# A shared pool of eight PSUM banks, and exp on VectorE for some score banks, in a fused attention and gated-MLP kernel

## The chip, the cores and the metric

The kernel runs on one core of a Trainium2 chip. The metric is device time in microseconds (us); lower is better. The engines are named as in the profile: PE is TensorE, ACT is ScalarE, DVE is VectorE, POOL is GpSimd, SP issues most of the DMAs. In the profile PE's weight loads stand under their own name, PEld, and overlap with PE.

## The reference

One pre-LN block, in bf16, for 2048 tokens of width 1024: attention with 32 query heads of width 32 that share one key and one value head, then a gated MLP of width 3584.

```
def _A_ref(x, wq, wk, wv, wo):              # H = 32 heads, Dh = 32
    q = (x @ wq).reshape(B, S, H, Dh).transpose(0, 2, 1, 3)
    k = x @ wk ; v = x @ wv                 # one head each
    p = softmax(einsum("bhqd,bkd->bhqk", q, k) * Dh ** -0.5)
    o = einsum("bhqk,bkd->bhqd", p, v)
    return o.transpose(0, 2, 1, 3).reshape(B, S, H * Dh) @ wo
def _B_ref(x, w_gate, w_up, w_down):
    return (sigmoid(x @ w_gate) * (x @ w_up)) @ w_down
h  = x + _A_ref(layernorm(x), ...)
h2 = h + _B_ref(layernorm(h), ...)
```

## The kernel before

A small planner inside the kernel lays out one fixed instruction order for each engine. It keeps a clock for each engine from constants for what an instruction costs, and gives PE at each step the work that it believes to be ready. On the chip every engine then runs its list in order.

PE's work is of two kinds. A *score visit* is 16 matmuls into four PSUM banks, followed by two exps of 1024 columns on ACT, which write probabilities into `Pr`. There are 512 visits, 32 for each tile of 128 queries. The *other work* fills PE between visits: transposes of x (xT), projections of Q, K and V, probabilities times V (PV), output projection (OP), gate/up (GU) and down (D). Score banks and banks for other work are separate tensors:

```python
S_ps = EC(nc.psum_tensor("S_ps", [P, 6, 512], F32))     # three pairs for scores
F_ps = EC(nc.psum_tensor("F_ps", [P, 2, 512], F32))     # two banks for other work
...
def emit_S(v):
    ... # 16 matmuls of 128 columns, four row groups of the array at a time
    for i in range(2):
        ...
        exps[u] = pl.op("act", lambda slot=slot, pb=pb: ACT.activation(
            out=Pr[:, slot, :].rearrange("p (a b) -> p a b", a=2), in_=S_ps[:, pb:pb + 2, :],
            func=ACTF.Exp, scale=SCALE), [last] + ..., prio=3, **t_act(1024))
```

The rule for PE (cut): a visit goes first when ACT has under 750 ns of work left; otherwise the one open group of other work continues; a new group is chosen only when none is open.

```python
if can_s and run - t < 750.0:
    emit_S(v) ...
if cur is not None:
    fn, n, deps = cur[1][cur_i]            # next matmul of the open group
    ...
else:
    pick = None
    for cl in PRIO:                        # xT, KV, Q0, PV, OP, D, GU, Q
        ...
```

Q beyond the first 512 tokens is staged in `hact`, the buffer that gate/up writes later, so gate/up starts only after all of Q is stored (`q_left[0] == 0`). While PE waits for input at the start it runs 76 dummy matmuls.

The softmax here doesn't subtract the row's maximum and nothing guards it: scores larger than these inputs give would overflow.

Of the kernel before, what the change touches and what calls it, by code (L numbers as in the profile page):

```python
# [8 lines left out]
F32 = mybir.dt.float32  # L9
ACTF = mybir.ActivationFunctionType  # L10
ALU = mybir.AluOpType

P = 128
DH = 32
LN_EPS_BF16 = 1.0013580322265625e-05
SEM = 75.0

# [110 lines left out]
def bass_sequential_preLN__grouped_kv_mqa__glu_gated_glu__prompt_kernel(  # L128
# [24 lines left out]
    KB = 4  # L153
    VPG = NT // KB
    NPS = 16
    NB = 3
    NSLAB = 5
    SW = 256
    VS = 34
    xf = A_x[0]  # L160
    of = out[0]

    with ExitStack() as es:
# [9 lines left out]
        Pr = SB("Pr", [NPS, 1024])  # L173
# [7 lines left out]
        xres = SB("xres", [2, D])  # L181
# [3 lines left out]
        tnh = SB("tnh", [3, 256], F32)  # L185
# [10 lines left out]
        S_ps = EC(nc.psum_tensor("S_ps", [P, 6, 512], F32))  # L196
        F_ps = EC(nc.psum_tensor("F_ps", [P, 2, 512], F32))
# [18 lines left out]
        qst = hact[:, :].rearrange("p (a b) -> p a b", b=512)  # L216
        NQS = NFT * 256 // 512
# [17 lines left out]
        def both(out_ap, in_ap):  # L235
# [8 lines left out]
            pattern=[[-1, P]], channel_multiplier=1), [c2], occ=300)  # L244
        c_w = pl.op("dve", lambda: DVE.memset(hact[:, 0:512], 0.0), occ=150)
# [93 lines left out]
        bank_rel = [[], []]  # L339
# [11 lines left out]
        def mk_xT(t):  # L351
            def atoms(b):
                tp = F_ps[:, b, :].bitcast(BF16)
                return [(lambda dt=dt: PE.transpose(out=tp[:, dt * P:(dt + 1) * P],
                                                    in_=x_sb[:, t, dt * P:(dt + 1) * P], identity=ident[:, :]),
                         P, []) for dt in range(DT)]

            def after(b, last):
                src = F_ps[:, b, :].bitcast(BF16).rearrange("p (a b) -> p a b", a=DT)
                fa, fd = both(xnT4[t // 4][:, :, (t % 4) * P:(t % 4 + 1) * P], src)  # L360
                xT_ev[t] = pl.op("act", fa, [last], prio=2, **t_act(1024))
                xT_pe[t] = last
                queue_after_xT(t)
                if t == NPT - 1:
                    for k in range(NPT, NT):
                        dma_xT(k)
                return [xT_ev[t]]
# [31 lines left out]
        def mk_KV(p):  # L399
            def atoms(b):  # L400
                r = []
                for dt in range(DT):
                    r.append((mm(F_ps[:, b, 0:256], wk4[:, dt, :], xnT(dt, p * 256, 256), dt == 0, dt == DT - 1),
                              256, rep_ops if dt == 0 else []))
                for k in range(2):
                    for dt in range(DT):
                        r.append((mm(F_ps[:, b, 256 + k * DH:256 + (k + 1) * DH],
# [4 lines left out]
            def after(b, last):  # L412
                fa, fd = both(kT4[:, p * 256:(p + 1) * 256], F_ps[:, b, 0:256])
                k_ev[p] = evac(fa, fd, 256, [last], 1)
                fa, fd = both(Vaug[:, 2 * p:2 * p + 2, 0:DH],
                              F_ps[:, b, 256:256 + 2 * DH].rearrange("p (a b) -> p a b", a=2))
# [9 lines left out]
        def mk_Q(g, tok, n):  # L426
            def atoms(b):
                return [(mm(F_ps[:, b, 0:n], wq_sb[:, dt, g * P:(g + 1) * P], xnT(dt, tok, n),
                            dt == 0, dt == DT - 1), n, []) for dt in range(DT)]

            def after(b, last):
# [4 lines left out]
                if n == 256:  # L436
                    fa, fd = both(QTb[:, tok // 256, g, :], F_ps[:, b, 0:256])
                    ev = evac(fa, fd, 256, [last], 1 if tok == 0 else 4)
                    q_ready[tok // 256][g] = ev
                else:  # L440
# [3 lines left out]
                    fa, fd = both(qst[:, s, :], F_ps[:, b, :])  # L444
# [48 lines left out]
        visits = []  # L493
        for gg in range(0, NT * NG, 2):
            if gg == 0:
                for kq in range(VPG):
                    visits += [(0, kq), (1, kq)]
            else:
                for q in (gg, gg + 1):
                    visits += [(q, kq) for kq in range(VPG)]  # L500
        NV = len(visits)
        exps = {}
        slot_of = {}
        slot_owner = {}
        pv_done = {}
        n_exp_of = collections.Counter()

        def s_ready(v):
            G, kq = visits[v]
            qb, g = G // NG, G % NG  # L510
            c = qb // 2
            if g not in q_ready[c]:
                return None
            if any(p not in k_ev for p in (2 * kq, 2 * kq + 1)):
                return None
            for i in range(2):
                own = slot_owner.get((2 * v + i) % NPS)
                if own is not None and own not in pv_done:
                    return None
            deps = [q_ready[c][g], k_ev[2 * kq], k_ev[2 * kq + 1]]  # L520
            if 2 * v - 2 >= 0:
                deps.append(exps[2 * v - 2])
            return deps

        def emit_S(v):
            G, kq = visits[v]
            qb, g = G // NG, G % NG
            c, qo = qb // 2, (qb % 2) * P
            deps = s_ready(v)
            pl.free["pe"] += 95.0  # L530
            last = None
            for kk in range(KB):
                for j in range(4):
                    kt = kq * KB + kk
                    bank = 2 * ((2 * v + j // 2) % NB) + j % 2
                    last = pl.op("pe", mm(S_ps[:, bank, kk * P:(kk + 1) * P], kT4[DH * j:DH * (j + 1), kt * P:(kt + 1) * P],
                                          QTb[DH * j:DH * (j + 1), c % 2, g, qo:qo + P], True, True,
                                          tile_position=(DH * j, 0)),
                                 deps if (kk == 0 and j == 0) else [], occ=15.0, lat=15.0 + 170.0 + SEM)
            pl.free["pe"] += 95.0  # L540
            for i in range(2):
                u = 2 * v + i
                slot = u % NPS
                own = slot_owner.get(slot)
                slot_owner[slot] = G
                slot_of[(G, kq, i)] = slot
                pb = 2 * (u % NB)
                exps[u] = pl.op("act", lambda slot=slot, pb=pb: ACT.activation(  # L548
                    out=Pr[:, slot, :].rearrange("p (a b) -> p a b", a=2), in_=S_ps[:, pb:pb + 2, :],
                    func=ACTF.Exp, scale=SCALE), [last] + ([pv_done[own]] if own is not None else []), prio=3, **t_act(1024))  # L550
                exp_of[(G, kq, i)] = exps[u]
            n_exp_of[G] += 1
            if G % (2 * NG) == 2 * NG - 1 and n_exp_of[G] == VPG:
                chunk_last_S[c] = last
                load_q(c + 2)
            if n_exp_of[G] == VPG:
                queues["PV"].append(mk_PV(G))

        exp_of = {}
# [3 lines left out]
        def mk_PV(G):  # L563
            qb, g = G // NG, G % NG
            def atoms(b):
                r = []
                for j in range(4):
                    for kt in range(NT):
                        kq, kk = kt // KB, kt % KB
                        slot = slot_of[(G, kq, j // 2)]  # L570
                        co = (j % 2) * 512 + kk * P
                        r.append((mm(F_ps[:, b, j * VS:j * VS + DH + 1], Pr[:, slot, co:co + P], Vaug[:, kt, 0:DH + 1],
# [3 lines left out]
            def after(b, last):  # L576
# [3 lines left out]
                ov = F_ps[:, b, 0:4 * VS].rearrange("p (a b) -> p a b", a=4)  # L580
# [14 lines left out]
            first = lambda: ([exp_of[(G, kq, i)] for kq in range(VPG) for i in range(2)] +  # L595
# [15 lines left out]
        def load_xr(t, deps):  # L611
            if t < NT:
                xr_ld[t] = dma(lambda: SP.dma_start(xres[:, t % 2, :], xf[t * P:(t + 1) * P, :]), f"xr{t % 2}", P * D * 2,
# [4 lines left out]
        def mk_OP(t, dc):  # L618
            def atoms(b):
                return [(mm(F_ps[:, b, :], OT[:, t % 2, g, :],  # L620
                            wo_sb[:, g, dc * 512:(dc + 1) * 512], g == 0, g == NG - 1), 512, []) for g in range(NG)]

            def after(b, last):
                sl = slice(dc * 512, (dc + 1) * 512)
                h_ev[(t, dc)] = pl.op("dve", lambda: DVE.tensor_tensor(  # L625
                    out=h_sb[:, t % 4, sl], in0=F_ps[:, b, :], in1=xres[:, t % 2, sl], op=ALU.add),
                    [last, xr_ld[t]] + ([out_dma[(t - 4, dc)]] if t >= 4 else []), prio=1, **t_dve(512))
                if dc == 1:
                    op_last[t] = last
                    load_xr(t + 2, [h_ev[(t, 0)], h_ev[(t, 1)]])  # L630
# [6 lines left out]
            gr.gate = lambda: len(wo_ld) == 2 and t in xr_ld and (t < 4 or (t - 4, dc) in out_dma) and (t < 2 or (t - 2) in hT_ev)  # L637
# [37 lines left out]
        def mk_GU(c, ft):  # L675
# [5 lines left out]
            def atoms(b):  # L681
                r = []
                for w in range(2):
                    for dt in range(DT):
                        r.append((mm(F_ps[:, b, w * 256:w * 256 + n], wgu[:, sl, w, dt, fo:fo + P], hnT[:, dt, 0:n],
# [3 lines left out]
            def after(b, last):  # L689
                k = n_gu[0] % 3  # L690
                n_gu[0] += 1
                a = pl.op("act", lambda: ACT.activation(out=tnh[:, k, 0:n], in_=F_ps[:, b, 0:n], func=ACTF.Tanh, scale=0.5),  # L692
# [4 lines left out]
                else:  # L697
                    deps += q_store[-NQS:]
                e = pl.op("dve", lambda: DVE.scalar_tensor_tensor(  # L699
                    out=hactT[:, ft, 0:n], in0=tnh[:, k, 0:n], scalar=1.0, in1=F_ps[:, b, 256:256 + n], op0=ALU.add,  # L700
# [13 lines left out]
            gr.gate = lambda: s in slab_ld and (q_left[0] == 0 if c == 0 else d_done[c - 1] == 2 * len(CH[c - 1]))  # L714
# [4 lines left out]
        def mk_D(c, t, dc):  # L719
# [3 lines left out]
            def atoms(b):  # L723
                return [(mm(F_ps[:, b, :], hactT[:, ft, tt * P:(tt + 1) * P], wd_sb[:, ft, dc * 512:(dc + 1) * 512],
                            ft == 0, ft == NFT - 1), 512, [ev[ft]] if tt == 0 and dc == 0 else []) for ft in range(NFT)]

            def after(b, last):
# [4 lines left out]
                    out=h_sb[:, t % 4, sl], in0=F_ps[:, b, :], scalar=0.5, in1=h_sb[:, t % 4, sl],  # L732
                    op0=ALU.mult, op1=ALU.add), [last], prio=2, **t_dve(512))
                out_dma[(t, dc)] = dma(lambda: SP.dma_start(of[t * P:(t + 1) * P, sl], h_sb[:, t % 4, sl]),
                                       f"o{t % 4}{dc}", P * 1024, [e], prio=2)
                return [e]
            return Group("D", atoms, lambda: list(wd_ld) + [ev[ft] for ft in range(NFT - 6)], after)
# [4 lines left out]
        for t in range(2):  # L742
            load_xr(t, [xnorm[NT - 1]])

        cur = None
        cur_i = 0
        cur_b = None
        v = 0
        idle = 0

        def known(deps, t):
            return all(d is not None and d.end is not None and d.end <= t for d in deps)

        while True:
            t = pl.free["pe"]
            pl.advance(t)
            if v < NV:
                run = max(pl.free["act"], t) + sum(o.occ for o in pl.heap["act"])
                sd = s_ready(v)
                can_s = sd is not None and known(sd, t)  # L760
                if can_s and run - t < 750.0:
                    emit_S(v)
# [152 lines left out]
```

## Time and profile before

| reading | value | view |
|---|---|---|
| time | 1198.2 us median of 4 (1195.8 to 1199.4) | |
| PE busy | 1169.7 us, 98% of the span | page, part 1 |
| ACT busy | 1043.8 us, 87% | page, part 1 |
| visit 192 begins | 427 us; PE idle since the first visit 20.9 us, ACT 20.1 us | gaps of the trace |
| last exp ends | 1072.6 us; then 124 us of matmuls without exps | gaps, chain of waits |

These are lines of the page of the kernel before: busy time by engine, then the span in 40 slices (a digit is tenths busy, PEclk is the granted clock in tenths), then the chain of work that ended last.

```profile
span 1196.8 us, 47622 instructions
...
PE 1169.7 (98%) x22204; PEld 830.8 (69%) x22204; DVE 293.6 (25%) x799; ACT 1043.8 (87%) x1312; POOL 38.5 (3%) x84
...
PE   9999988999999999999999999999999999999999
...
ACT  6899989999999999999999999999999999981120
...
PEclk9999989999999999999999999999999999999999
...
PE 88%; ACT 6%; issue 2%; DVE 2%; DMA 2%; SPq 0%; ACTq 0%; DVEq 0%
```

After the start PE and ACT are both near full up to slice 36; then ACT falls off and PE goes on. The chain is 88% PE: PE ends last. PE's only visible dents are at slices 6 and 7, the clock's is at slice 6.

Groups of instructions by form, on ACT. After the bar: busy time in us, mean duration of one in ns, and idle time before them with what ended it.

```profile
L548 ACT ACTIVATE Pr<-S_ps 128x1024 bf16<-128x1024 f32 x1024 | 977.5, 1042 | 28.5 <-PE S_ps L349 27.7
L692 ACT ACTIVATE tnh<-F_ps 128x256 f32<-128x256 f32 x196 | 77.1, 393 | 82.4 <-PE F_ps L349 82.4
```

The mean of 1042 ns is longer than an exp costs, because the records of neighbours overlap. The cost is the distance from one start to the next without idle time between: 903 to 920 ns in the trace.

The timeline around 148 us shows the dent (start, duration, engine, line, what; in brackets the idle time before it and what ended it).

```profile
146.72 7.53 ACT L548 ACTIVATE Pr<-S_ps 128x1024 bf16<-128x1024 f32 x8
...
147.88 0.40 PE L349 MATMUL S_ps<-QTb,kT 32*128 32x128 bf16 x16 [1.40 <-ACT Pr L548]
...
149.72 0.61 PE L349 MATMUL S_ps<-QTb,kT 32*128 32x128 bf16 x16 [1.43 <-ACT Pr L548]
...
151.55 0.61 PE L349 MATMUL S_ps<-QTb,kT 32*128 32x128 bf16 x16 [1.22 <-ACT Pr L548]
```

ACT works without a break here, and PE has only score visits left: it stands still until ACT empties a bank.

### The profile page before, as it was taken

How to read it: one execution, taken by the hardware profiler on the slowest of the kernel's cores; microseconds unless marked ns; L12 is line 12 of the kernel's file. 1: busy time of each engine (PE TensorE's matmuls, PEld its weight loads, DVE VectorE, ACT ScalarE, POOL GpSimd, SP SyncE). 2: the span in 40 equal slices, each digit the busy share in tenths (PEclk: the TensorE clock that was granted, in tenths of full speed). 3: DMA queues.
4: the chain of work that ended last, by engine and by line, in shares of the span. 5: the costliest groups of instructions: out<-in, count | busy, mean ns of one | idle time of the engine just before them, and what ended most of it. 6: DMA issues, size and time to landing. Idle time of an engine off the chain costs nothing.

```text
span 1196.8 us, 47622 instructions
## 1 busy us (share of the span) xinstructions
PE 1169.7 (98%) x22204; PEld 830.8 (69%) x22204; DVE 293.6 (25%) x799; ACT 1043.8 (87%) x1312; POOL 38.5 (3%) x84
## 2 busy tenths in 40 slices
PE   9999988999999999999999999999999999999999
PEld 5755567677577856787577856777568765786684
DVE  8423212121213121221212221213122221222121
ACT  6899989999999999999999999999999999981120
POOL 4100000000000000000000000000000000000000
PEclk9999989999999999999999999999999999999999
DMA  8665499489456632667155650666226750479480
GB/s 241 161 182 155 138 280 242 107 210 286 82 142 160 178 90 55 163 177 182 29 122 151 194 118 12 159 178 178 64 64 178 187 139 15 117 192 228 123 208 18
DMA packets 332021, 176.74 MB, mean 148 GB/s; under 512 B 52016, under 2 KB 322352, under 8 KB 331824
## 3 DMA queue, kind: packets, MB, share of 16 engines
q1 hardware_dynamic: 329744, 173.57, 55.6%
q8 instruction: 174, 2.85, 1.0%
q10 hardware_dynamic: 2080, 0.13, 0.1%
q14 instruction: 23, 0.19, 0.0%
HBM read 155.32 MB, written 7.34 MB: 136 GB/s over the span
## 4 chain that ended last, share of the span: by engine, by line
PE 88%; ACT 6%; issue 2%; DVE 2%; DMA 2%; SPq 0%; ACTq 0%; DVEq 0%
PE F_ps L349 75%; PE S_ps L349 13%; ACT Pr L548 5%; DMA q_scratch<-hact 1%; ACT tnh L692 1%; DVE st L290 0%; DMA ring<-in_A_x_dram 0%; DVE st L292 0%; DMA zone<-ring 0%; DVE ring L329 0%; ACT ring L333 0%; DVE hact L699 0%; DVE ring L336 0%; ACT zone L236 0%; DVE mv L294 0%
## 5 line engine op out<-in xcount | busy, mean ns | idle before, releaser
L548 ACT ACTIVATE Pr<-S_ps 128x1024 bf16<-128x1024 f32 x1024 | 977.5, 1042 | 28.5 <-PE S_ps L349 27.7
L349 PE MATMUL F_ps<-hnT,ring 128*128 128x256 bf16 (+1 forms) x4032 | 446.9, 263 | 5.1 <-issue 4.2
L349 PEld LDWEIGHTS F_ps<-hnT,ring 128*128 128x128 bf16 x4032 | 342.6, 98 | 62.9 <-issue 8.9
L349 PEld LDWEIGHTS F_ps<-Vaug,Pr 128*128 128x128 bf16 x8192 | 229.2, 96 | 29.1 <-issue 3.7
L349 PE MATMUL F_ps<-Vaug,Pr 128*128 128x33 bf16 x8192 | 244.2, 177 | 3.7 <-issue 1.9
L349 PE MATMUL S_ps<-QTb,kT 32*128 32x128 bf16 x8192 | 208.4, 218 | 11.0 <-ACT Pr L548 7.3
L349 PE MATMUL F_ps<-zone,hact 128*128 128x512 bf16 x896 | 213.7, 380 | 0.0
L349 PEld LDWEIGHTS S_ps<-QTb,kT 32*128 32x128 bf16 x8192 | 119.3, 93 | 124.2 <-ACT Pr L548 73.7
L699 DVE SCALAR_TENSOR_TENSOR hact<-tnh,F_ps 128x256 bf16<-128x256 f32 (+1 forms) x252 | 97.7, 391 | 439.5 <-ACT tnh L692 431.3
L692 ACT ACTIVATE tnh<-F_ps 128x256 f32<-128x256 f32 (+1 forms) x252 | 93.9, 378 | 86.2 <-PE F_ps L349 86.2
L349 PEld LDWEIGHTS F_ps<-zone,hact 128*128 128x128 bf16 x896 | 78.8, 98 | 88.0
L349 PE MATMUL F_ps<-zone 128*128 128x256 bf16 (+2 forms) x512 | 75.4, 289 | 2.0 <-ACT QTb L236 1.4
L731 DVE SCALAR_TENSOR_TENSOR h_sb<-F_ps,h_sb 128x512 bf16<-128x512 f32 x32 | 22.1, 691 | 204.7 <-PE F_ps L349 204.7
L349 PE MATMUL F_ps<-wo_sb,OT 128*128 128x512 bf16 x256 | 65.0, 384 | 0.6 <-issue 0.6
L581 DVE RECIPROCAL rL<-F_ps 128x4 f32<-128x4 f32 x128 | 23.3, 182 | 140.1 <-PE F_ps L349 140.0
L349 PEld LDWEIGHTS F_ps<-zone 128*128 128x128 bf16 x512 | 37.3, 97 | 23.7 <-ACT QTb L236 1.6
L304 POOL TENSOR_SCALAR zb<-mvb 128x1 bf16<-128x1 bf16 (+1 forms) x25 | 5.6, 225 | 1046.9 <-DVE mvb L300 1046.9
L583 DVE TENSOR_TENSOR Osb<-F_ps,rL 128x128 bf16<-128x128 f32 x128 | 37.3, 291 | 4.2
L349 PEld LDWEIGHTS F_ps<-wo_sb,OT 128*128 128x128 bf16 x256 | 22.1, 99 | 23.0 <-issue 1.9
L625 DVE TENSOR_TENSOR h_sb<-F_ps,xres 128x512 bf16<-128x512 f32 x32 | 22.1, 691 | 47.2 <-PE F_ps L349 47.2
L237 DVE CAST hact<-F_ps 128x512 bf16<-128x512 f32 x24 | 16.6, 691 | 38.2 <-PE F_ps L349 38.1
L349 PE MATMUL S_ps<-hact,ident 128*128 128x512 bf16 x76 | 19.8, 411 | 1.8 <-POOL ident L242 1.8
(36 smaller groups left out, 154.8 us busy)
## 6 DMA issues: line engine op xcount, KB each, us to landing
ring<-in_B_w_gate_dram SPq DMA_DIRECT2D x126, 512.0 KB, 4.3
ring<-in_B_w_up_dram SPq DMA_DIRECT2D x126, 512.0 KB, 6.0
zone<-in_B_w_down_dram SPq DMA_DIRECT2D x7, 1024.0 KB, 8.5
xres<-in_A_x_dram SPq DMA_DIRECT2D x16, 256.0 KB, 2.8
out_dram<-h_sb SPq DMA_DIRECT2D x32, 128.0 KB, 1.7
q_scratch<-hact SPq DMA_DIRECT2D x24, 128.0 KB, 2.8
QTb<-q_scratch SPq DMA_DIRECT2D x6, 512.0 KB, 5.0
ring<-in_A_x_dram SPq DMA_DIRECT2D x5, 512.0 KB, 6.8
```

The costliest lines, as they stand in the source:

```text
L237: lambda: DVE.tensor_copy(out=out_ap, in_=in_ap))
L304: f = pl.op("pool", lambda: POOL.tensor_scalar(out=zb[:, ph, sl].unsqueeze(2), in0=mvb[:, ph, sl, 1:2], scalar1=LN_EPS_BF16, scalar2=None, ...
L349: return lambda: PE.matmul(o, lhsT=l, rhs=r, start=start, stop=stop, **kw)
L548: exps[u] = pl.op("act", lambda slot=slot, pb=pb: ACT.activation(out=Pr[:, slot, :].rearrange("p (a b) -> p a b", a=2), in_=S_ps[:, pb:pb ...
L581: a = pl.op("dve", lambda: DVE.reciprocal(rL[:, k, :].unsqueeze(2), ov[:, :, DH:DH + 1]), [last], prio=0, occ=70, lat=280)
L583: e = pl.op("dve", lambda: DVE.tensor_tensor(out=Osb[:, qb % 2, g * P:(g + 1) * P].rearrange("p (a b) -> p a b", a=4), in0=ov[:, :, 0:DH], ...
L625: h_ev[(t, dc)] = pl.op("dve", lambda: DVE.tensor_tensor(out=h_sb[:, t % 4, sl], in0=F_ps[:, b, :], in1=xres[:, t % 2, sl], op=ALU.add), [ ...
L692: a = pl.op("act", lambda: ACT.activation(out=tnh[:, k, 0:n], in_=F_ps[:, b, 0:n], func=ACTF.Tanh, scale=0.5), [last, tn_user.get(k)], pri ...
L699: e = pl.op("dve", lambda: DVE.scalar_tensor_tensor(out=hactT[:, ft, 0:n], in0=tnh[:, k, 0:n], scalar=1.0, in1=F_ps[:, b, 256:256 + n], op ...
L731: e = pl.op("dve", lambda: DVE.scalar_tensor_tensor(out=h_sb[:, t % 4, sl], in0=F_ps[:, b, :], scalar=0.5, in1=h_sb[:, t % 4, sl], op0=ALU ...
```

## The change

Its intent: ease ACT in the first third, where PE runs out of other work, and give PE more freedom everywhere. It has these parts.

1. One pool of eight banks. A visit takes any four free ones, other work may hold up to three (`FMAX`). Where two free banks are neighbours one exp covers both (1024 columns), otherwise each gets its own (512).
2. In the first 400 us of the plan the fourth bank of some visits goes to VectorE: six instructions that build exp from exponent bits and a cubic. These come out as exp(x)/(16·K3), so the exps on ACT get a bias of −log(16·K3).
3. Q gets two staging buffers of its own, so gate/up can start early and is mixed with Q.
4. Two groups of other work may be open; xT, KV, PV and OP may break into an open group. A visit goes first when ACT has under 1000 instead of 750 ns left.
5. `x` is loaded straight into `h_sb`; down waits until all its weights are issued; `tnh` has two buffers instead of three.

The diff, cut to its core:

```diff
+K3 = 0.07802452
+EXP_LN = -math.log(16.0 * K3)
-    NPS = 16
-    NB = 3
+    NPS = 32
+    T_DVE = 400e3
+    FMAX = 3
-        S_ps = EC(nc.psum_tensor("S_ps", [P, 6, 512], F32))
-        F_ps = EC(nc.psum_tensor("F_ps", [P, 2, 512], F32))
+        PS = EC(nc.psum_tensor("PS", [P, 8, 512], F32))
+        c_e = pl.op("pool", lambda: POOL.memset(ebias[:, :], EXP_LN), [c_id], occ=60)
...
-                    out=Pr[:, slot, :].rearrange("p (a b) -> p a b", a=2), in_=S_ps[:, pb:pb + 2, :],
-                    func=ACTF.Exp, scale=SCALE), [last] + ..., prio=3, **t_act(1024))
+                w = 2 if i % 2 == 0 and free[i + 1] == free[i] + 1 and not (i == 2 and off) else 1
+                ex = pl.op("act", lambda b=free[i], w=w, slot=slot: ACT.activation(
+                    out=Pr[:, slot * 512:(slot + w) * 512], in_=PS[:, b:b + w, :].rearrange("p a b -> p (a b)"),
+                    func=ACTF.Exp, scale=SCALE, bias=ebias[:, 0:1]), ..., prio=3, **t_act(512 * w))
...
-            gr.gate = lambda: s in slab_ld and (q_left[0] == 0 if c == 0 else ...)
+            gr.gate = lambda: s in slab_ld and (True if c == 0 else ...)
...
+        URGENT = ("xT", "KV", "PV", "OP")
+            if banks and len(active) < 2 and f_use < (FMAX if v else 6):
+                order = PRIO[:-2] + ["Q", "GU"] if q_left[0] * GQ > NFT - n_gu[0] else PRIO
...
+            if new is not None and (not go or (new[0] in URGENT and RANK[new[0]] < RANK[go[0][0].cls])):
+                gr = queues[new[0]].popleft()      # breaks into the open group
```

The compiled order says what came of it: 46 of 2048 banks on VectorE, 830 exps of 1024 and 342 of 512 columns on ACT, 52 dummies, and otherwise the same matmuls.

## The prediction

> **What bounds the kernel now.** The page: span 1196.8 us, PE busy 1169.7 (98%), ACT 1043.8 (87%), DVE 293.6 (25%). By windows of 50 us: until the last exp ends at 1072 us ACT is mostly 94 to 99% busy and PE nearly as much; then comes a tail of matmuls alone (the chain of waits ends in one piece of 123.6 us). So PE ends last, and time saved on ACT helps only where PE waits. That is the first third: between the first score matmul (27.7) and 427 us PE is idle 21 us and ACT 19.5; from 427 on PE is idle under 2. The timeline shows why: near 147 to 155 score matmuls wait for exp with no other work placed between (gate/up waits for all of Q to be projected and stored; q_scratch<-hact is 9.5 us of the chain), near 172 PE waits 2.1 us for a weight slab while the DMA share is 0.96 to 1.05. There the granted clock reads 0.90, 0.93, 0.97: about 10 us of array time lost. The Trainium skill ("TensorE: Matmul & The Clock Gate", Part 1) says that low activity over a window of about 3.4 us halves the clock; the trace agrees that the drops stand only behind this gappy stretch.
>
> **What the change does, from the compiled order.**
> - Matmuls stay but for 24 of 76 warm-up dummies (0.214 us each): 5 us. Score visits stay separate (508 runs, then 506), so PE's cost of entering and leaving them stays.
> - Q staging no longer shares gate/up's output buffer: 336 gate/up matmuls instead of 32 lie in the first 64 visits, which spreads the slabs and fills PE's gaps.
> - Only 46 of 2048 score banks go to VectorE, all by about visit 190 (six instructions each; a 128x512 PSUM read takes 0.69 us here, so I estimate 3.5 us a bank, 160 in all, which DVE can hold).
> - ACT: 1024 exps of 1024 columns become 830 and 342 of 512. Back to back a 1024 takes 0.93 us (8 in 7.44); at 0.833 ns a column I estimate 0.505 for a 512. Sum 953 before, 946 after: splits give back most of the 21 us that VectorE takes.
>
> **Critical path.** Up to visit 192 (427 us before): PE without its idle, 5 us of dummies and 5 of slow clock would end near 396; ACT without 21 us and most of its idle near the same. Both never close fully: 403 to 407. After that PE is saturated in both and nothing changes; the tail shrinks by 84 gate/up matmuls (9 us) that only moved forward; the 1.5 us per 64 visits that splits cost ACT hides under PE.
>
> **Prediction.** 1199.4 - 22 = 1177 us, range 1165 to 1192. Faster by over 2%: 0.43; within 2%: 0.54; slower by over 2%: 0.03.
>
> **Right if:** PE idle before 430 us falls from 21 to under 8; clock drops mostly gone; visit 192 comes 18 to 26 us earlier; the tail after the last exp is about 112 us; the later pace per 64 visits stays within 2 us of 129; DVE about 38% busy.
>
> **Wrong if:** score visits now need four free banks of a shared eight while other work may hold three: ACT could starve, or the 512-column exps cost more than 0.505, and PE then idles in the middle, giving the gain back. VectorE's chains could delay the attention output's normalisation and so PE. Better if PE stays filled beyond what I assume.

## More of the kernel before

What the planner believes of a DMA, such as the transpose `OT<-Osb` that the output projection waits for, is a constant start-up and a rate:

```python
go = max(s + 1300.0, self.dma_free[e])
self.dma_free[e] = go + o.nbytes / 280.0
o.end = self.dma_free[e] + 700.0
```

## The result, and the profile after

The changed kernel took 1265.05 us (median of 4, 1263.3 to 1265.9) against 1198.17: a ratio of 1.0559, 95% interval 1.0536 to 1.0582. A ratio here is the mean time of one kernel's runs over that of the kernel before in the same rounds, so it is not quite the ratio of the medians quoted. The prediction said 1177, at most 1192.

The page after, the same lines:

```profile
span 1263.7 us, 48236 instructions
...
PE 1198.9 (95%) x22180; PEld 818.7 (65%) x22180; DVE 434.4 (34%) x1071; ACT 1129.9 (89%) x1464; POOL 41.4 (3%) x85
...
PE   9899997998899999999999999999999999999999
...
ACT  7899999998999999999999999999999999994020
...
PEclk9999997999899999999999999999999999999999
...
ACT 59%; PE 30%; issue 5%; DVE 3%; DMA 1%; POOL 1%; POOLq 0%; ACTq 0%; DVEq 0%
```

The chain has changed hands: 59% ACT where it was 6%. ACT's busy time rose by 86 us although it has less to compute. The same groups on ACT:

```profile
L621 ACT ACTIVATE Pr<-PS,ebias 128x1024 bf16<-128x1024 f32 x830 | 907.4, 1261 | 17.8 <-PE PS L363 16.6
L621 ACT ACTIVATE Pr<-PS,ebias 128x512 bf16<-128x512 f32 x342 | 257.8, 841 | 0.0
L770 ACT ACTIVATE tnh<-PS 128x256 f32<-128x256 f32 x196 | 108.1, 552 | 75.7 <-PE PS L363 75.7
```

An exp of 1024 columns has a mean of 1261 instead of 1042 ns, and there is a second input in its name: `ebias`. From start to start the trace has 996 ns where it had 903 to 920, and 569 ns for 512 columns. The longest pieces of the chain of waits (start, length, what) run through ACT in stretches of 39 to 56 us; only the last is PE's tail. After the last exp 115 us remain, against 124 before; the loss lies in front of it.

```profile
595.56 38.97 ACT Pr L621 x42
725.71 55.72 ACT Pr L621 x64
...
1027.82 46.41 ACT Pr L621 x47
1154.89 105.90 PE PS L363 x734
```

PE's busy time rose too, by 29 us with 24 matmuls fewer. That is waiting in disguise: a matmul's modelled end runs up to the next start if that is near. From visit 192 on, the distance from the last gate/up matmul to the score visit behind it is 205 ns at the median and at the 90th percentile before; after, it is 293 and 445. Summed over all entries into visits, the excess over the 10th percentile is 0.1 us before and 25.4 us after, beside the idle gaps (24.3 us in the whole span before, 61.9 after). The Trainium skill ("Trainium Kernel Development and Optimization", Performance Expectations) calls matmul busy time a bad metric for how close a kernel is to roofline, because matmuls are pipelined; this trace agrees, since those 25.4 us of waiting stand in it as work.

### The profile page after: what moved, and what is told of

Read it like the earlier page. It is cut to its first block, busy times and chain, and to the rows that moved or that the text cites. A ratio compares the mean times of both kernels' runs of the same rounds, so it can differ in the third digit from the quotient of the medians.

```text
span 1263.7 us, 48236 instructions
## 1 busy us (share of the span) xinstructions
PE 1198.9 (95%) x22180; PEld 818.7 (65%) x22180; DVE 434.4 (34%) x1071; ACT 1129.9 (89%) x1464; POOL 41.4 (3%) x85
## 4 chain that ended last, share of the span: by engine, by line
ACT 59%; PE 30%; issue 5%; DVE 3%; DMA 1%; POOL 1%; POOLq 0%; ACTq 0%; DVEq 0%
ACT Pr L621 56%; PE PS L363 30%; ACT tnh L770 3%; DVE hact L777 1%; DVE st L303 0%; DMA OT<-Osb 0%; DMA zone<-ring 0%; DMA q_scratch<-qst 0%; DVE ez L568 0%; POOL rstd L324 0%; DVE st L305 0%; DVE h_sb L704 0%; POOL dsb L322 0%; DVE et L579 0%; DVE rL L660 0%
## 5 line engine op out<-in xcount | busy, mean ns | idle before, releaser
L621 ACT ACTIVATE Pr<-PS,ebias 128x1024 bf16<-128x1024 f32 (+1 forms) x1172 | 1082.5, 1139 | 17.8 <-PE PS L363 16.6
L363 PE MATMUL PS<-hnT,ring 128*128 128x256 bf16 (+1 forms) x4032 | 448.1, 262 | 2.5 <-issue 1.8
L363 PEld LDWEIGHTS PS<-hnT,ring 128*128 128x128 bf16 x4032 | 338.8, 98 | 63.9 <-issue 5.3
L363 PEld LDWEIGHTS PS<-Vaug,Pr 128*128 128x128 bf16 x8192 | 223.7, 96 | 66.7 <-issue 25.3
L363 PE MATMUL PS<-Vaug,Pr 128*128 128x33 bf16 x8192 | 246.8, 178 | 14.7 <-ACT Pr L621 6.1
L363 PE MATMUL PS<-QTb,kT 32*128 32x128 bf16 x8192 | 210.4, 219 | 38.7 <-ACT Pr L621 18.6
L363 PEld LDWEIGHTS PS<-QTb,kT 32*128 32x128 bf16 x8192 | 122.2, 93 | 170.7 <-ACT Pr L621 114.4
L363 PE MATMUL PS<-zone,hact 128*128 128x512 bf16 x896 | 220.0, 382 | 0.5 <-issue 0.5
L777 DVE SCALAR_TENSOR_TENSOR hact<-tnh,PS 128x256 bf16<-128x256 f32 (+1 forms) x252 | 98.2, 391 | 347.9 <-ACT tnh L770 347.4
L770 ACT ACTIVATE tnh<-PS 128x256 f32<-128x256 f32 (+1 forms) x252 | 125.1, 498 | 77.8 <-PE PS L363 77.7
L809 DVE SCALAR_TENSOR_TENSOR h_sb<-PS,h_sb 128x512 bf16<-128x512 f32 x32 | 22.1, 690 | 87.3 <-PE PS L363 87.3
L568 DVE TENSOR_SCALAR ez<-PS 128x512 uint32<-128x512 f32 x46 | 31.8, 691 | 57.4 <-PE PS L363 57.1
L704 DVE TENSOR_TENSOR h_sb<-PS,h_sb 128x512 bf16<-128x512 f32 x32 | 22.1, 691 | 56.4 <-PE PS L363 56.3
```

Of the source, the lines that this page charges most:

```text
L363: return lambda: PE.matmul(o, lhsT=l, rhs=r, start=start, stop=stop, **kw)
L568: z = pl.op("dve", lambda: DVE.tensor_scalar(out=ez[:, :], in0=PS[:, b, :], scalar1=SCALE * math.log2(math.e) * 2.0 ** 23, scalar2=123.0 * ...
L621: ex = pl.op("act", lambda b=free[i], w=w, slot=slot: ACT.activation(out=Pr[:, slot * 512:(slot + w) * 512], in_=PS[:, b:b + w, :].rearran ...
L704: h_ev[(t, dc)] = pl.op("dve", lambda: DVE.tensor_tensor(out=h_sb[:, t % 4, sl], in0=PS[:, b, :], in1=h_sb[:, t % 4, sl], op=ALU.add), [la ...
L770: a = pl.op("act", lambda: ACT.activation(out=tnh[:, k, 0:n], in_=PS[:, b, 0:n], func=ACTF.Tanh, scale=0.5), [last, tn_user.get(k)], prio= ...
L777: e = pl.op("dve", lambda: DVE.scalar_tensor_tensor(out=hactT[:, ft, 0:n], in0=tnh[:, k, 0:n], scalar=1.0, in1=PS[:, b, 256:256 + n], op0= ...
```

## The experiments

There were 17. All gave correct results. "Constant bias" means the line of e1. PE idle is the sum of the gaps in PE's matmul records over the span; for e13 to e17 it is left out, since some 100 of the 22,180 records are missing in those traces and each leaves a false gap.

| run | what it is | median us | ratio to before (95%) | PE idle us |
|---|---|---|---|---|
| after | the change | 1265.1 | 1.0559 (1.0536 to 1.0582) | 61.9 |
| e1 | constant bias | 1211.5 | 1.0137 (1.0092 to 1.0183) | 38.2 |
| e2 | before, column bias added | 1261.5 | 1.0529 (1.0498 to 1.0560) | 58.4 |
| e3 | after, no exp on VectorE | 1272.7 | 1.0630 (1.0604 to 1.0656) | 65.9 |
| e4 | e1, no exp on VectorE | 1207.0 | 1.0072 (1.0045 to 1.0099) | 36.2 |
| e5 | e1, other work holds two banks | 1230.7 | 1.0245 (1.0208 to 1.0282) | 45.9 |
| e6 | e1, fixed 6+2 banks | 1224.4 | 1.0202 (1.0170 to 1.0234) | 47.1 |
| e7 | e6, no exp on VectorE | 1211.7 | 1.0092 (1.0061 to 1.0124) | 36.6 |
| e8 | after, planner told of the bias | 1293.3 | 1.0788 (1.0743 to 1.0833) | 93.3 |
| e9 | e7, one open group, 750 ns | 1199.6 | 1.0010 (0.9979 to 1.0040) | 28.0 |
| e10 | e7, Q before gate/up | 1213.6 | 1.0114 (1.0091 to 1.0138) | 38.0 |
| e11 | e9 and e10 together | 1195.5 | 0.9974 (0.9946 to 1.0001) | 26.3 |
| e12 | e1, one open group, 750 ns | 1196.1 | 0.9973 (0.9949 to 0.9996) | 28.5 |
| e13 | e1, one open group | 1203.8 | 1.0029 (1.0005 to 1.0053) | |
| e14 | e1, 750 ns | 1214.9 | 1.0130 (1.0106 to 1.0154) | |
| e15 | e12, no exp on VectorE | 1206.8 | 1.0054 (1.0033 to 1.0075) | |
| e16 | e12, Q before gate/up | 1203.5 | 1.0023 (0.9995 to 1.0051) | |
| e17 | e1, OP may not break in | 1200.3 | 1.0013 (0.9984 to 1.0043) | |

### First: does the column bias cost the time? (e1 to e4)

My theory after reading the two traces was the new operand. The Trainium skill ("ScalarE: Activation LUTs", What ACT_TABLE_LOAD costs) says that each [128,1] pointer operand adds about 93 ns to an ACTIVATE; I had not looked it up for the prediction. The rivals were PSUM reads slowed by the pool or by VectorE, and the 512-column splits.

e1, one operand:

```diff
-  func=ACTF.Exp, scale=SCALE, bias=ebias[:, 0:1]), ...
+  func=ACTF.Exp, scale=SCALE, bias=EXP_LN), ...
```

> The changed kernel with one operand altered: the bias of the 1172 exps is a constant in the instruction instead of a [128,1] column of SBUF. Instruction order on every engine is identical to the changed kernel. Theory (the column bias costs each exp about 76 to 93 ns of ACT, start to start 996 instead of 903 to 920 for 1024 columns, 569 instead of an estimated 490 for 512; 1172 of them make 90 to 105 us): exps fall to 905-920 and 480-500 ns start to start, the time to 1165 to 1190 us. Rivals (the shared bank pool or the VectorE work slows ACT's reads of PSUM; or the 512-column splits are what costs): exps stay at 996 and 569 and the time stays within 1% of 1265.

It took 1211.5 us, 54 us less, with the same order on PE, ACT and VectorE. Groups on ACT in e1:

```profile
L621 ACT ACTIVATE Pr<-PS 128x1024 bf16<-128x1024 f32 x830 | 810.0, 1040 | 45.0 <-PE PS L363 42.6
L621 ACT ACTIVATE Pr<-PS 128x512 bf16<-128x512 f32 x342 | 199.3, 621 | 0.0
```

From start to start exps are back at 905 and 478 ns (427 ns for 512 columns, so the prediction's 0.833 ns a column was right). So the operand costs 91 ns an exp at either width, and 1172 of them make 107 us of ACT's time. ACT's busy total fell by 89 us (1129.9 to 1040.9); part of that went into ACT waiting for PE, and the end came 54 us sooner. The time missed the expected range of 1165 to 1190: something else was wrong too.

e2, the kernel before with a column of zeros (`bias=ebias[:, 0:1]` on its 1024 exps):

> The kernel before with only a column of zeros as bias of its 1024 exps (same numbers, same order on PE). Theory: start to start goes from 903-920 to about 996, so ACT gets 78 to 95 us more work on a PE order that is fixed; ACT's 20 us of idle in the first third takes up a little, the tail stays about 121 us; time 1255 to 1285 us. Rival (bank pool): within 1% of 1198.

It took 1261.5 us, a ratio of 1.0529 with no pool, no VectorE, no split. The group line (exps of the kernel before with the column):

```profile
L550 ACT ACTIVATE Pr<-S_ps,ebias 128x1024 bf16<-128x1024 f32 x1024 | 1081.1, 1358 | 16.5 <-PE S_ps L351 16.5
```

The operand is enough to bring about nearly all of the loss. 996 ns start to start again.

e3 and e4 take the exps off VectorE (`T_DVE = 0.0`), with either bias.

> The changed kernel, column bias kept, without any exp on VectorE (829 exps of 1024 and 390 of 512 columns on ACT instead of 830 and 342). Theory: ACT has 48 more 512-column exps at 569 ns, 27 us, and is what bounds the kernel now: 1280 to 1300 us. Rival (VectorE's reads of PSUM slow the rest): the time falls under 1255.

> Constant bias and no exp on VectorE: the shared pool alone. Theory: PE bounds, ACT carries 24 us more than in e1 in the first third, where PE then waits a little; 1180 to 1205 us, that is 5 to 20 us over e1. If VectorE's part is worth nothing even with a cheap bias it is within 4 us of e1.

e3 was slower than the changed kernel (1272.7), though less than I expected; so VectorE's part does not slow the rest. e4 surprised me: without VectorE's exps it was as fast as e1 or faster (1.0072 against 1.0137, intervals that just overlap). In the profiled runs its last score visit begins 19 us later than in e1 (1108 against 1089 us), and yet its end comes only 2 us later. Attention that finishes sooner had bought nothing.

### Second: are the banks to blame for the rest? (e5 to e8)

In e1, ACT idles 34.3 us from the first visit to visit 192, against 20.1 before (the expectation of e5 says 35.7 and 19.5). I took the banks to be the reason.

e5: `FMAX = 3` becomes `FMAX = 2`.

> e1 (constant bias) with at most two of the eight banks for the other work instead of three (the limit that the kernel before has by its fixed split). Theory: with three banks out, a score visit finds its four free banks only when ACT has a single bank left, 478 ns, less than the visit needs to deliver; so ACT starved for 35.7 us by visit 192 in e1 against 19.5 before, and single banks had to be taken, 342 exps of 512 columns. Here the order has 975 exps of 1024 and 50 of 512. ACT idle to visit 192 under 25 us, and the time 1180 to 1200 us, below e1 by over 10. Rival (the idle of PE comes from work that the attention chain has not yet set free, and from late instruction fetch and DMA, not from banks): PE idle stays 30 us or more and the time within 5 us of e1's 1211.

e6 undoes the pool for scores, e7 takes VectorE's exps away as well:

```diff
-            pairs = [b for b in free if b + 1 in free]
+            pairs = [b for b in (0, 2, 4) if b in free and b + 1 in free]    # both pairs or no visit
...
-            banks = [b for b in range(8) if bank_free(b, t)]
+            banks = [b for b in (range(6, 8) if v else range(8)) if bank_free(b, t)]
```

> e1 with the shared pool undone: score visits take pairs of banks 0 to 5, other work banks 6 and 7, as before; VectorE still computes 48 banks. Theory (banks cost the rest): like e5, 1180 to 1200 us. Rival: within 5 us of e1.

> As e6 with no exp on VectorE: 1024 exps of 1024 columns as before. What is left of the change is the Q staging, the earlier gate/up and two interleaved groups. If these are worth the 5 us of dummies and some idle that I had assumed: 1185 to 1197 us. If VectorE's 48 banks matter, e6 is 5 to 15 us under this one; if PE work is all that counts the two agree within 4 us.

My theory fell. e5 and e6 are slower than e1. They did what I had asked for: in e5 visit 192 begins at 405.5 us, right where my prediction had put it, and the last visit 48 us before e1's. But 896 gate/up matmuls are then left for the tail instead of 558. These are lines of e5's page:

```profile
span 1224.2 us, 47935 instructions
...
PE 1175.4 (96%) x22180; PEld 827.4 (68%) x22180; DVE 445.8 (36%) x1086; ACT 1022.9 (84%) x1314; POOL 39.1 (3%) x85
...
ACT  7799899999999999999999999999997999111120
```

ACT's last exp ends at 1044 us, 29 us sooner than in the kernel before, and yet the end comes later: PE idles 45.9 us. The time of the runs follows PE's work and its waits; the work (PE's time from start to start without the gaps) is 1161 to 1175 us in all constant-bias runs with complete records.

e8 tells the planner nearly the truth about the changed kernel's exps (`t_act(512 * w + 96)`, which is 80 of the 91 ns more) and leaves the column bias in.

> The changed kernel with its column bias, but the planner that lays out PE's order is told 80 ns more for each exp. Theory: in the changed kernel PE waits hidden in front of score visits (as in e2, 30 us of it from visit 192 on) because its order was laid out for a faster ACT, while work that could fill them lies in the tail; told the truth, the tail shrinks from 558 to 448 gate/up and 224 to 122 down matmuls (34 us of PE): 1225 to 1250 us, though exps stay at 996 and 569. Rival (ACT alone sets the time): within 8 us of 1265.

It was slower still, 1293.3 us. The tail did shrink, to 100 us from the last visit to the end against 118, but PE now runs dry at every pair of query tiles. The page, and the timeline of PE around one of these places:

```profile
span 1290.3 us, 48200 instructions
...
PEclk9899978997699999999899988999899998999799
...
612.99 0.40 PE L363 MATMUL PS<-QTb,kT 32*128 32x128 bf16 x16 [0.83 <-ACT Pr L621]
614.91 0.40 PE L363 MATMUL PS<-QTb,kT 32*128 32x128 bf16 x16 [1.52 <-ACT Pr L621]
...
626.45 0.40 PE L363 MATMUL PS<-QTb,kT 32*128 32x128 bf16 x16 [1.61 <-ACT Pr L621]
...
633.50 3.21 PE L363 MATMUL PS<-hnT,ring 128*128 128x256 bf16 x16
...
641.41 2.14 PE L363 MATMUL PS<-hnT,ring 128*128 128x256 bf16 x18
```

Work for a pair of tiles becomes available only when attention has finished them. Used up early, it is missing later: PE waits for exps with nothing beside them, the clock drops to half (from 615.7 to 619.1 and from 629.3 to 636.1 us in its records), and 16 gate/up matmuls take 3.21 us where 18 take 2.14 at full clock. PE spent 141 us of this run at half clock, 22 before. So both of my ideas about e8 were wrong: it was neither a gain nor a standstill, but a loss.

### Third: the planner's rules (e9 to e14 and e17)

e9 gives e7 the old rules: `len(active) < 1` instead of `< 2`, and 750 instead of 1000 ns. e10 gives it the old order of Q and gate/up. e11 has both. e12 gives e1 the old rules and keeps pool and VectorE.

> e7 (constant bias, fixed 6+2 banks, no exp on VectorE) with one group of other work open at a time, and a score visit put first only when ACT has under 750 ns left, as in the kernel before; the earlier gate/up and the Q staging stay. Theory by now: the end is set by PE's work plus what PE waits (before 1169 + 24 us, e1 1167 + 38, e5 1175 + 46), and finishing attention earlier earns nothing. If the two open groups and the 1000 ns rule make PE wait, PE idle falls from e7's 36 us to under 30 and the time to 1195 to 1205 us. Rival (the early gate/up is at fault): within 4 us of e7's 1211.7.

> e7 with the order of Q and gate/up as before (gate/up waits until all of Q is projected). Theory: the amount of other work that the attention chain has set free by visit 128 is the same in either order, so moving gate/up forward only moves the place where PE starves: within 5 us of e7. Rival (the early gate/up itself costs): 1195 to 1205 us. Rival the other way (the early gate/up is worth what I predicted): over 1220 us.

> e9 and e10 together: what is left against the kernel before is the Q staging in its own two buffers, x loaded straight into h, all eight banks in use before the first score visit (54 dummies instead of 76) and the constant bias. Expected: 1190 to 1200 us, within 1% of the kernel before; if the 5 us of dummies are worth what I gave them, 3 to 6 us under it.

> e1 (shared pool, 46 banks on VectorE or so, constant bias) with one open group and the 750 ns rule. If these two rules are what makes PE wait, 1192 to 1204 us; if the pool does, 1207 to 1216, like e1.

The rules were it: e9 gained 0.8 points of ratio over e7, and e12 1.6 over e1 (each pair on two chips; e13 and e14 below shared one). e10 did not differ from e7: moving gate/up forward is worth nothing there. e12 keeps the pool and VectorE's exps and comes out 0.3% under the kernel before, at the edge of what can be told. Lines of its page:

```profile
span 1192.3 us, 48004 instructions
...
PE 1161.0 (97%) x22183; PEld 826.9 (69%) x22183; DVE 433.7 (36%) x1067; ACT 1037.2 (87%) x1364; POOL 41.6 (3%) x85
...
PE 94%; ACT 3%; DMA 1%; issue 1%; DVE 0%; POOL 0%; POOLq 0%
```

PE's busy time is 8.7 us under that of the kernel before: some 5 of it are dummies replaced by early work. PE's idle time, 28.5 us, is no better than the 24.3 before.

e13 and e14 take the two rules apart.

> e1 with one open group alone, the score rule left at 1000 ns. If the second open group is what costs e1 its 15 us against e12: within 3 us of e12's 1196. If the 1000 ns rule does: near e1's 1211.

> e1 with the 750 ns rule alone, two open groups left. The mirror of e13: near 1211 if the second open group costs, near 1196 if the 1000 ns rule does; both in between if each has a part.

The second open group costs (e14 1.0130, e13 1.0029), the 1000 ns rule nothing between e14 and e1, and up to 0.6 points between e13 and e12; both of these pairs ran on different chips. Without permission to break in, the program with two groups is instruction for instruction that of e13, so breaking in is all that the second group does. e17 takes the permission from the output projection alone:

```diff
-        URGENT = ("xT", "KV", "PV", "OP")
+        URGENT = ("xT", "KV", "PV")
```

> e1 with the output projection no longer allowed to break into an open group (the attention-times-V groups still are). Without either permission the program is instruction for instruction e13, so breaking in is all that the second open group does. PE's gaps before output projections are 6.4 us in e1 and 0.6 before; if it is they, near e13's ratio of 1.003; if it is attention-times-V breaking in (with 354 single-bank exps still, against 136 in e13), near e1's 1.014.

It is enough: 1.0013. The output projection of a tile waits for a DMA transpose, `OT<-Osb`. e1's timeline shows what breaking in does (SPq is a DMA issue; the transpose is issued at 959.72):

```profile
959.72 2.10 SPq L668 DMA_TRANSPOSE OT<-Osb  x1
...
963.46 0.83 PE L363 MATMUL PS<-hnT,ring 128*128 128x256 bf16 x6
...
966.41 2.04 PE L363 MATMUL PS<-wo_sb,OT 128*128 128x512 bf16 x5 [2.12 <-ACT Pr L621]
```

PE stops in the middle of a gate/up group of 16 after six matmuls, stands for 2.12 us, and resumes 0.1 us after the transpose has landed. The view names ACT as the releaser; the DMA's own record is what fits. These transposes took 3.0 to 7.0 us from issue to landing in e1, where the planner assumes 2.9 (worked out from its constants for 256 KB). In e1 and in e4, 12 of the 16 output projections start within 0.2 us of the landing, that is, PE had been waiting for it; before, in e13 and in e17, none (in e13 and e17 by the first matmul that has a record); in e12, two. In the changed kernel, where ACT holds PE up anyway, it is five. With one group open the planner's optimism did not matter: the output projection had to let a group finish first, which gave the DMA its time. The gaps before output projections sum to 6.4 us in e1, 0.6 before and 0.3 in e12. The profiled spans of e1 and e12 differ by 16.6 us: 9.7 are PE's idle time, 6.8 the sum of PE's slots. In one place the wait also cost clock: behind the 2.12 us the record shows half clock from 966.7 to 970.1 us. How the rest of the loss follows from the waits I have not shown. A direct test, which keeps the permission and gives the planner a longer DMA latency, was not run. Nor does this account cover the fixed banks: the gaps before output projections sum to 2.0 us in e7 and 2.2 in e9, so what the old rules saved there is not shown.

### Fourth: is VectorE's part worth anything, and is there a better mix? (e15, e16)

> e12 without exps on VectorE (982 exps of 1024 and 84 of 512 columns on ACT). e12's gain over the kernel before is 3 us with PE's idle time by visit 192 still 26 us, so I expect VectorE's part to be worth little: within 4 us of e12, most likely 1 to 4 us slower. My prediction's idea (ACT relief in the first third shortens PE's wait) would make it 10 us or more slower.

> e12 with Q projected before gate/up begins, as before: the candidate to beat both kernels. e11 against e9 gave 4 us for it with the fixed banks; here 1190 to 1196 us. If early gate/up is worth anything it is slower than e12.

Against e12, e15 is 0.8 points slower, about 10 us, and the intervals are apart; but the two ran on different chips. In e15's own call e13 and e16, with VectorE's exps, are 0.3 points faster, with intervals that overlap or touch. Each of those two also differs from e15 in one other rule. So a gain of 0.3% to 0.8% from VectorE's part, once the output projection no longer breaks in, is likely but not shown, and in e1 and e4 there is none to see. e16 was to beat e12 and did not. e11 and e12, 0.3% under the kernel before, are the best kernels; neither is faster by a margin that matters.

## Why the prediction was wrong, point by point

The prediction was 1177 us; 88 us are missing. Three steps of the sum failed.

| step of the prediction | said | found | us |
|---|---|---|---|
| "at 0.833 ns a column I estimate 0.505 for a 512. Sum 953 before, 946 after" | no cost for the bias | 91 ns an exp at both widths (e1); 512 columns take 478 ns without it, 569 with it; sum 1021 after (830 of 996 and 342 of 569 ns) | 54 (1265.1 to 1211.5) |
| "After that PE is saturated in both and nothing changes" | same pace, 129 us per 64 visits | 140.5 in the changed kernel, 132.4 without the column (e1), 129.0 in e12: output projections break into open groups before their DMA has landed (e17, e12) | 15 (1211.5 to 1196.1) |
| "403 to 407" for visit 192, so 22 us off the end | PE idle before 430 us from 21 to under 8 | 33.0 us in the changed kernel (visit 192 at 444.5 us, 31 us at half clock where it was 22); 27.1 in e1, 26.1 in e12, 22.1 in e11 | 19 (1196.1 to 1177) |

The split follows the order in which the parts were taken out: added to the kernel before, the column alone costs 63 us (e2).

**The missed operand.** The prediction counted exps and columns and did not see that `bias=ebias[:, 0:1]` makes each exp dearer. It listed "the 512-column exps cost more than 0.505" as a danger, for no reason that it knew. With the bias the chain of waits runs through ACT up to the tail, so PE was no longer what set the pace. That is the mechanism of the loss, and e1 and e2 show it from both sides.

**The slack that went.** The prediction read the compiled order for counts, not for what the new rules let happen between a DMA and the matmul behind it. The danger that it named, visits starved of banks by the third bank of other work, was tried in e5 and e6; taking that bank away made it worse.

**The gain that never came.** This is the step that the prediction was built on. It took the time of visit 192 as a milestone of progress. e5 reached it at 405.5 us, as predicted, but by luck: PE had been idle 30.4 us by then, not under 8. It was slower, because the other work that belongs to those visits had been put off. What counts is PE's work and PE's waits. The work fell as said: with 52 to 55 instead of 76 dummies the sum of PE's slots in e12 is 8.7 us smaller. The waits did not fall. The run of visits without other work at 148 us before has moved to 196 and 319 us in e1. I think that the reason is that the other work that attention has set free by a given visit is the same in any order; e10 (no difference) and e8 (the work used early, missing later) agree with it, but no run shows a schedule that is free of the wait or that it must stay, so this remains open. Nor is it settled why e12's idle time to visit 192 is 26 us where e11's is 22.

**What was right.** The matmul counts, the 46 banks on VectorE and their cost (3.5 us estimated; the six instructions sum to 3.59 us in the group lines of the changed kernel), that VectorE's exps would not hinder anything, the tail (112 us predicted after the last exp; 115 after, 117 in e1), and that PE bounds the kernel before: from visit 192 on it has neither gaps over 1.5 us in all nor hidden waits.

## What to carry to other kernels

Cost every operand of an instruction that is repeated a thousand times, not only its size, and read ACT's cost from start to start rather than from mean durations. Where PE ends last, judge a schedule by PE's work and PE's waits, hidden ones in front of each dependent matmul included; a milestone that comes earlier because other work was put off is no gain. In a fixed order, permission to start urgent work at once needs a DMA latency with room to spare: in e1 PE stood 2.12 us behind one such wait with ten matmuls of its gate/up group left.

## What the Trainium skill lacked or had wrong

- "ScalarE: Activation LUTs" (What ACT_TABLE_LOAD costs): the step for a [128,1] operand, about 93 ns, agrees (91 ns measured at 512 and at 1024 columns). The page's absolute figures do not fit these exps, which read PSUM and write bf16: 186 ns plus 0.833 ns a column, less 93 ns of overlap, gives an estimate of 946 ns for 1024 columns and 519 for 512; measured are 905 and 478, and with the operand 996 and 569 where the page's figures give 1040 and 614. The skill has the PSUM figure elsewhere, in "Perfetto Trace Analysis" (Optimizing Scalar/DVE Operations): about 51 ns of overhead for a ScalarE instruction on PSUM, which with 0.833 ns a column gives an estimate of 904 and 478 ns and fits.
- "TensorE: Matmul & The Clock Gate" (the table of why this matters for your kernels): its rule is no PE-idle gaps over about 3 us. In e8 the clock fell to half at 615.7 us behind gaps of at most 1.52 us: 0.56, 0.60, 0.83 and 1.52 us within the 7.3 us before. Several short gaps close together were enough. In e1 one gap of 2.12 us (ending at 966.4 us) was followed by half clock and one of 2.13 us (at 1100.1 us) was not. Both fit the same page's account in Part 1, of a free-running activity window and of a kernel that short idle times kept throttling, better than its rule.
- No page that I found gives the spread of an SBUF-to-SBUF DMA transpose under load: 256 KB took 3.0 to 7.2 us from issue to landing within one run of the kernel before.
- "Runtime: NRT & Kernel Launch" (Instruction fetch mechanics) says that an engine's instructions come in blocks of 16 KiB and that crossing into the next block is mostly hidden; it gives no case of PE waiting there in straight-line code. PE's gaps over 1 us that the profile calls "issue" mostly stand 1.2 to 1.5 us behind the end of a 16 KB packet of the instruction queue (both such gaps of the kernel before in the first third, 172.3 and 208.1 us; in e1 those at 57.1, 135.8, 152.8 and 265.9 us); the packets end 6.7 us apart on average. The prediction took the gap at 172.3 us for a wait for a weight slab; the profile names no releaser. The nearness to the packets is a coincidence in time, not shown as a cause.
